# Small-tile matmuls grouped by kind, POOL used throughout, and a new set of plan numbers, in a window-attention and feed-forward kernel

## The chip, the cores and the metric

One NeuronCore of a Trainium2 chip runs the whole kernel. Its engines are TensorE (PE, with its weight loads as PEld), VectorE (DVE), ScalarE (ACT), GpSimd (POOL) and SyncE (SP, which here issues all DMAs). The metric is the device time of one execution in microseconds (us), the median of several runs.

## The reference

Attention with a window of 32 positions and 32 global rows, for 8 batches of 8 heads, and on its output a feed-forward block. Cut to what is computed:

```python
batch, n_heads, seq_l, seq_g, head_dim = (8, 8, 512, 32, 64)
...
s_g = scale * np.matmul(q_g, k_all.transpose(0, 1, 3, 2))
out_g = np.matmul(sm(s_g), v_all)                 # 32 global rows see everything
mask = np.abs(pos[:, None] - pos[None, :]) <= 32
s_ll = np.where(mask, scale * np.matmul(q_l, k_l.transpose(0, 1, 3, 2)), -1000000000.0)
s_l = np.concatenate([scale * np.matmul(q_l, k_g.transpose(0, 1, 3, 2)), s_ll], axis=-1)
out_l = np.matmul(sm(s_l), np.concatenate([v_g, v_l], axis=2))
x = concat(out_g, out_l) as (8 * 544, 512)
h = x @ w_in                                      # 512 -> 2048
sp = np.maximum(h, 0.0) + np.log1p(np.exp(-np.abs(h)))
return ((h * erf(sp)) @ w_out).astype(np.float32)
```

The weights w_in and w_out come as 64-bit floats.

## The kernel before

The kernel doesn't write its instructions in order. It records steps (`add`, with the engines that may take a step, a duration for each, a key, what is read and written, and for PE the number of instructions), and `Program.schedule` lays them out: event by event, each free engine takes from its ready steps the one of lowest key whose buffers are free. The keys are counted in units of the feed-forward work and come from the table of numbers at the head of the file (HKEYS for the heads, GATE, PROJ, KEEP and so on for the rest). The schedule's order is then what each engine runs. Steps marked for DVE and POOL may go to POOL only where their key lies in SHARED; `elsewhere` decides between two engines that may take a step, `crowded` holds back PE steps of many small instructions, and `filler` puts warming matmuls (spare) into PE's row early on where it would be idle.

*Attention.* Heads go in pairs that share q and k. For a pair PE makes the scores of both heads (s, 64 matmuls, tiles of 64x32 in the array); for each head DVE adds the mask and takes row maxima into sm and mx, ACT takes the exponential (for the first BIASED heads with the maximum as its bias, four instructions; later DVE or POOL subtracts it and ACT needs one), PE transposes (t, full 128x128), ACT or DVE copies (pt), PE multiplies with the values (o, 32 matmuls, tiles of 128x32), and DVE divides by the row sum (rs, xn). After a pair, xn is transposed (xT) and stored to DRAM (xsc). After every four heads come the same steps for the 32 global rows (ga, gb scores; pg; gt; go values; gx; xsg). Batch 0 takes a shorter way into the feed-forward block (`straight`, tiles x).

*Feed-forward, first 768 columns.* For each batch c (and chunk 8, the global rows) six units h of 12 matmuls: each product of fp32 numbers is three matmuls of rounded halves (xh with winh, xl with winh, xh with winl). ACT copies h to hs and takes softplus and erf in groups of AG units into sp; DVE or POOL multiplies by hs; gh is the rounded half and gl the rest; PE projects (op, from gh, gl with wouth, woutl) and the partial sums go to DRAM (part). The w_in and w_out blocks are first turned from 64-bit to 32-bit floats by integer steps on DVE (top_in, top_out), and for the other 1,280 columns written back to DRAM (`keep_in`, `keep_unit`: top_l_in, part, top_k_out, hi_k_out, lo_k_out).

*Feed-forward, the other columns.* Batches in pairs: seven block products per unit in place of eight (pa to pd, weights wq), folded by DVE and ACT (u, c, pair), then the same gate and projection, with part added on DVE (os) and the rows stored. The first of these products comes after all attention; behind the last attention step PE has full-array matmuls alone.

In the trace 32 matmuls make one head's values and 64 a pair's scores; all PE matmuls are recorded at line 344 and transposes at 345, ACT at 346, DVE and POOL at 356, and DMAs at 348, since helpers record them.

Of the kernel before, what the change touches and what calls it, by code (L numbers as in the profile page):

```python
# [21 lines left out]
P = 128  # L22
# [7 lines left out]
CROWD, STRETCH, EVADE = 254, 4.013, 0.27  # L30
# [3 lines left out]
HKEYS = ((0, -5.063), (10, -3.503), (22, 0.608), (64, 30.894))  # L34
STEP, GKEY = 0.023, -0.868
QLEAD, VLEAD, RLEAD, XLEAD = 0.459, 0.046, 0.011, 2.412
GOFF, POFF = 1.452, 1.865
WIN, WOUT = (-2.963, -1.41, -1.202), (3.958, 3.604, 3.417)
BIASED, AG = 30, 3
SHARED = (-99.0, 17.961)  # L40
TPAIR = 2.626
KEEP, KSTEP, FIRST = 16.147, 2.595, (-2.849, 0.951)
CVO = (50.84, 53.645, 53.996, 48.864, 55.397)
QLEAD2, XDEL, SLOTS = 10.999, 1.259, 11
GATE1, GATE2, PROJ1, PROJ2 = (3.909, 9.618, 11.922), (13.773, 23.579, 27.539), 17.617, 26.859
SPT = 0.35
BIAS, AHEAD = 1.072, 15.956
# [3 lines left out]
SLACK, PORT = {"PE": 0.8, "SP": 0.8}, 0.7  # L51

# [6 lines left out]
WLEAD = 0.011  # L59
LATER, GFIRST = 8, (-2.568, -2.486)  # L60
NORMAL = 1.125 * 2.0**-15
STRAIGHT, XLATE = True, -0.932
# [44 lines left out]
class Program:  # L107
# [9 lines left out]
    def add(self, ways, key, fn, reads=(), writes=(), moved=0.0, heat=0, ins=None):  # L117
# [9 lines left out]
        op.heat, op.ins = heat, ins or heat // 256  # L127
# [31 lines left out]
    def schedule(self):  # L159
# [28 lines left out]
        warmth, issued = [], []  # L188
# [13 lines left out]
        def fill():  # L202
            dur = fill_dur if now > COLD else 2 * fill_dur
            until["PE"] = max(since, now) + dur
            heapq.heappush(events, (until["PE"], -1, 0, None))
            if now >= since:
                op = Op()
                op.eng, op.ways, op.fn, op.key, op.start, op.heat = "PE", {"PE": dur}, fill_fn, 0.0, now, fill_heat
                op.new, op.bufs = [], []
                order.append(op)  # L210
                warmth.append((now, fill_heat))

# [6 lines left out]
        while events or any(o.eng is None for o in self.ops) and ahead < 1e3:  # L219
# [14 lines left out]
            while picked:  # L234
                picked = False
                for e, q in ready.items():
# [4 lines left out]
                    while until[e] <= now and (dense or q and q[0][0] <= line[front].key + ahead):  # L241
# [4 lines left out]
                        item = dense.pop(0) if dense_only and dense else heapq.heappop(q)  # L246
# [6 lines left out]
                        if any(free[k] < n for k, n in need.items()) or elsewhere(op, e):  # L253
# [22 lines left out]
                        dur = op.ways[e] + toll  # L276
                        if e == "DVE" and op.port:
# [28 lines left out]
def kernel(  # L306
# [109 lines left out]
    def attention(b, h, key):  # L416
# [17 lines left out]
        if h % 2 == 0:  # L434
# [39 lines left out]
        if biased:  # L474
            add({"ACT": 1.05}, key, exps, [TAB, MX], [SM])
# [16 lines left out]
        PT = abuf([P, 4, P], f"pt_{nm}", "pt", 2)  # L492
        add({"PE": 0.5}, key + STEP * 2, transposes, [SM, CS], [T, PT], heat=512, ins=8)
# [3 lines left out]
        def values():  # L497
# [10 lines left out]
        add({"PE": 0.64}, key + STEP * 3, values, [PT, VA, VB], [O], heat=1040, ins=64)  # L508
        RS = abuf([P, 4, 1], f"rs_{nm}", "rs", 2)
        add({"DVE": 0.07},  # L510
            key + STEP * 3,
            lambda: dve.tensor_scalar(RS.ap, O.ap[:, :, D : D + 1], 1e-9, None, op0=ALU.add),
            [O],
            [RS],
        )
        add({"DVE": 0.09}, key + STEP * 3, lambda: dve.reciprocal(RS.ap, RS.ap), [], [RS])

        def norm(e):
            if e == "DVE":
                dve.tensor_tensor(  # L520
                    XN.ap[:, :, r0 : r0 + D], O.ap[:, :, :D], RS.ap.to_broadcast([P, 4, D]), ALU.mult
                )
            else:
                for t in range(4):
                    act(XN.ap[:, t, r0 : r0 + D], O.ap[:, t, :D], AF.Copy, scale=RS.ap[:, t, :])

        add({"DVE": 0.34, "ACT": 0.85}, key + STEP * 3, norm, [O, RS], [XN])
# [20 lines left out]
        if h % 4 == 3:  # L548
# [191 lines left out]
    class View:  # L740
# [3 lines left out]
        def ap(self):  # L744
            return self.f(self.buf.ap)
# [624 lines left out]
```

## Time and profile before

| | before |
|---|---|
| median of 3 runs | 922.99 us (922.47 to 924.45) |
| span of the profiled execution | 920.8 us |
| PE busy | 897.3 us, 97% |
| weight loads (PEld) busy | 720.7 us, 78% |
| DVE busy | 667.2 us, 72% |
| ACT busy | 570.1 us, 62% |
| POOL busy | 61.7 us, 7% |
| HBM traffic | 203 GB/s over the span |

The span runs from the first to the last instruction of the profiled execution; the median of the runs lies 2.2 us above it. Busy times are of engines that overlap each other. A matmul's recorded duration overlaps that of the next, so the pace of PE is read from the starts of successive groups in the chain of waits. The page's share of the chain by line gives op 38%, h 12%, and pa to pd together some 21%.

### The profile page before, as it was taken

The numbers are of one execution on the slowest core, as the hardware profiler recorded it, in microseconds if no ns is written. First come the engines' busy times: TensorE is split into PE (matmuls) and PEld (weight loads), VectorE is DVE, ScalarE is ACT, GpSimd is POOL, SyncE is SP. The second block draws the span as 40 slices with busy tenths as digits, with TensorE's granted clock in tenths as the row PEclk, the third lists the DMA queues.
The fourth block names the chain that finished last, engine by engine and source line by source line (L and its number), as shares of the span: only waits on it lengthen the run. The fifth ranks groups of instructions, "written<-read, shape, count | busy, mean of one in ns | idle before, by whom it ended". The sixth has DMA issues, their size and how long they took to land.

```text
span 920.8 us, 22337 instructions
## 1 busy us (share of the span) xinstructions
PE 897.3 (97%) x8814; PEld 720.7 (78%) x8814; DVE 667.2 (72%) x1733; ACT 570.1 (62%) x975; POOL 61.7 (7%) x51
## 2 busy tenths in 40 slices
PE   8799989999999999999999999999999999999998
PEld 5576767777777778888888888888888888888886
DVE  4698989978979897768857867648674677445562
ACT  4578986656757676866855569425862476335760
POOL 0003543131100000000000000000000000000000
PEclk9899999999999999999999999999999999999999
DMA  9698986979697885823458953644355535455121
GB/s 338 224 305 265 317 270 214 301 240 285 213 313 252 274 281 177 293 110 124 151 204 299 343 181 124 217 139 154 89 183 173 193 91 159 126 170 167 66 80 68
DMA packets 110017, 188.23 MB, mean 204 GB/s; under 512 B 15576, under 2 KB 39384, under 8 KB 109912
## 3 DMA queue, kind: packets, MB, share of 16 engines
q1 hardware_dynamic: 109912, 186.79, 61.8%
q8 instruction: 70, 1.15, 0.5%
q14 instruction: 35, 0.29, 0.1%
HBM read 145.59 MB, written 41.16 MB: 203 GB/s over the span
## 4 chain that ended last, share of the span: by engine, by line
PE 84%; DMA 6%; DVE 6%; issue 2%; ACT 1%; SPq 1%; DVEq 0%; ACTq 0%
PE op L344 38%; PE h L344 12%; PE pd L344 6%; PE pc L344 6%; PE pa L344 6%; PE pb L344 3%; PE o L344 3%; PE t L345 3%; PE s L344 2%; DMA wq<-part 2%; PE h_g L344 2%; DMA vb<-in_vB_dram 1%; DMA xsc<-xT 1%; DMA k<-in_kE_dram 1%; PE gt L345 1%
## 5 line engine op out<-in xcount | busy, mean ns | idle before, releaser
L344 PE MATMUL op<-wouth,gh 128*128 128x512 f32 x544 | 215.9, 397 | 0.4 <-DVE mx L356 0.4
L344 PE MATMUL op<-wouth,gl 128*128 128x512 f32 x544 | 212.1, 390 | 0.2 <-issue 0.2
L344 PE MATMUL op<-woutl,gh 128*128 128x512 f32 x544 | 212.0, 390 | 0.0
L347 ACT ACT_TABLE_LOAD x108 | 138.6, 1283 | 2.7 <-PEq L1357 0.7
L344 PEld LDWEIGHTS op<-wouth,gh 128*128 128x128 f32 x544 | 102.2, 188 | 23.2 <-issue 2.0
L344 PEld LDWEIGHTS op<-wouth,gl 128*128 128x128 f32 x544 | 102.1, 188 | 21.8
L344 PEld LDWEIGHTS op<-woutl,gh 128*128 128x128 f32 x544 | 102.2, 188 | 19.6
L356 DVE TENSOR_TENSOR gl<-sp,gh 128x512 fp32r<-128x512 f32 x129 | 89.4, 707 | 27.8 <-ACT gh L346 18.3
L346 ACT ACTIVATE gh<-sp 128x512 fp32r<-128x512 f32 x94 | 57.2, 627 | 83.8 <-PE op L344 71.1
L344 PE MATMUL h<-xh,winh 128*128 128x512 f32 (+1 forms) x216 | 85.8, 397 | 0.3 <-ACT hs L346 0.3
L344 PE MATMUL h<-xh,winl 128*128 128x512 f32 (+1 forms) x216 | 82.5, 382 | 0.0
L344 PE MATMUL h<-xl,winh 128*128 128x512 f32 (+1 forms) x216 | 82.5, 382 | 0.0
L346 ACT ACTIVATE sp<-sp 128x512 f32<-128x512 f32 x136 | 75.9, 621 | 0.5
L356 DVE CUSTOM_DVE_ANT_0 sm<-s,cs 128x128 f32<-128x128 f32 x256 | 57.1, 283 | 12.2 <-DMA cs<-in_cst_dram 7.0
L344 PE MATMUL pa<-xh_B,wq 128*128 128x512 f32 x160 | 55.8, 389 | 0.0
L344 PE MATMUL pd<-xh_T,wq 128*128 128x512 f32 x160 | 55.6, 389 | 0.0
L346 ACT ACTIVATE hs<-h 128x512 f32<-128x512 f32 x44 | 26.0, 595 | 41.5 <-PE h L344 41.3
L344 PEld LDWEIGHTS h<-xh,winh 128*128 128x128 f32 x216 | 41.1, 190 | 9.3 <-issue 1.0
L356 DVE TENSOR_TENSOR pair<-u,pc 128x512 f32<-128x512 f32 x40 | 27.4, 684 | 27.6 <-PE pc L344 27.5
L344 PEld LDWEIGHTS h<-xh,winl 128*128 128x128 f32 x216 | 41.0, 190 | 8.0
L344 PEld LDWEIGHTS o<-va,pt 128*32 128x32 f32 x768 | 31.7, 109 | 19.1 <-issue 11.2
L344 PEld LDWEIGHTS h<-xl,winh 128*128 128x128 f32 x216 | 41.1, 190 | 6.7
(163 smaller groups left out, 1687.0 us busy)
## 6 DMA issues: line engine op xcount, KB each, us to landing
wq<-wq SPq DMA_DIRECT2D x140, 256.0 KB, 3.3
vb<-in_vB_dram SPq DMA_DIRECT2D x64, 325.0 KB, 5.2
rx<-xsc SPq DMA_DIRECT2D x30, 512.0 KB, 5.4
va<-in_vA_dram SPq DMA_DIRECT2D x64, 195.0 KB, 4.8
k<-in_kE_dram SPq DMA_DIRECT2D x32, 384.0 KB, 5.1
wq<-part SPq DMA_DIRECT2D x35, 256.0 KB, 4.3
q<-in_qT_dram SPq DMA_DIRECT2D x32, 272.0 KB, 4.9
part<-os SPq DMA_DIRECT2D x34, 256.0 KB, 3.4
```

The source lines that it names most:

```text
L344: pe = lambda n, *a, **k: pinned(nc.tensor.matmul(n, *a, **k))
L345: tr = lambda *a, **k: pinned(nc.tensor.transpose(*a, **k))
L346: act = lambda *a, **k: pinned(nc.scalar.activation(*a, **k))
L347: table = lambda name: pinned(nc.scalar.preload_act_table_set(name))
L356: return lambda *a, **k: pinned(f(*a, **k))
```

## The change

The diff gives `schedule` a notion of PE's form: every PE step has a mode (F for full tiles, S for scores, O for values), a change of mode adds a duration from TURN to the plan, and a PE that is in a small form picks the ready step of lowest key after taking NEAR off the keys of its own form. From head 18 on (PAIRED) the two heads' values are one step; from batch 6 on (GOJOIN, GSJOIN) the global values join the pair's values and the global scores join the scores of the second pair. SM and PT get four buffers in place of two. `normalize`, `global_scores`, `global_probs` and `global_rows` hold the former lines of `attention` and `attention_global`. SHARED ends at 151.646, beyond every key. BIASED goes from 30 to 44. Nearly all numbers of the table and many of the planned durations are new. Cut to its core:

```diff
-CROWD, STRETCH, EVADE = 254, 4.013, 0.27
+CROWD, STRETCH, EVADE = 254, 4.013, 0.46
-HKEYS = ((0, -5.063), (10, -3.503), (22, 0.608), (64, 30.894))
-STEP, GKEY = 0.023, -0.868
+HKEYS = ((0, -4.696), (12, -2.264), (22, 0.416), (64, 28.821))
+STEP, GKEY = -0.256, -4.361
...
-BIASED, AG = 30, 3
-SHARED = (-99.0, 17.961)
+BIASED, AG = 44, 3
+SHARED = (-99.0, 151.646)
...
-QLEAD2, XDEL, SLOTS = 10.999, 1.259, 11
+QLEAD2, XDEL, SLOTS = 4.0, -0.178, 10
...
+TURN = {"FS": 0.11, "FO": 0.11, "SF": 0.35, "OF": 0.28, "SO": 0.31, "OS": 0.30}
+NEAR = 2.684
+PAIRED, GOJOIN, GSJOIN, PTS = 17, 6, 6, 4
+SMS, SPARED = 4, 0
...
-STRAIGHT, XLATE = True, -0.932
+STRAIGHT, XLATE = True, 15.301
...
+                        elif e == "PE" and mode != "F" and NEAR:
+                            item = min(q, key=lambda i: (i[0] - (NEAR if i[2].mode == mode else 0.0), i[1]))
+                            q.remove(item)
+                            heapq.heapify(q)
...
+                        if e == "PE":
+                            dur += TURN.get(mode + op.mode, 0.0)
+                            mode = op.mode
...
-            add({"PE": 1.24}, key, scores, [Q, K], SS, heat=2048, ins=128)
+            if h % 4 == 2 and b >= GSJOIN:
+                GA, GB, more = global_scores(b, h // 4, [st["qk", 0], (Q, K)])
+                G0[b, h // 4] = GA, GB
+
+                def joint():
+                    scores()
+                    more()
+
+                add({"PE": 1.9}, key, joint, [*st["qk", 0], Q, K], [*SS, GA, GB, GTURN], heat=3136, ins=160, mode="S")
+            else:
+                add({"PE": 1.02}, key, scores, [Q, K], SS, heat=2048, ins=128, mode="S")
-        SM = abuf([P, 4, P], f"sm_{nm}", "s", 2)
+        SM = abuf([P, 4, P], f"sm_{nm}", "s", SMS)
...
-        PT = abuf([P, 4, P], f"pt_{nm}", "pt", 2)
+        PT = abuf([P, 4, P], f"pt_{nm}", "pt", PTS)
...
+        if h % 4 == 3 and b >= GOJOIN:
+            joined = global_probs(*group, key + GKEY)
+        if NH * b + h - h % 2 < PAIRED:
+            add({"PE": 0.55}, key + STEP * 3, values, [PT, VA, VB], [O], heat=1040, ins=64, mode="O")
+            normalize(O, XN, r0, nm, key)
+        elif h % 2 == 0:
+            st["o"] = values, [PT, VA, VB], O, r0, nm
+        else:
+            first, need, O0, *rest = st["o"]
+            last, more, GO = joined or (None, [], None)
+
+            def pair():
+                first()
+                values()
+                if last:
+                    last()
+
+            add({"PE": 1.11 + 0.72 * (GO is not None)},
+                key + STEP * 3,
+                pair,
+                [*need, PT, VA, VB, *more],
+                [O0, O] + [GO] * (GO is not None),
+                heat=2080,
+                ins=128 + 96 * (GO is not None),
+                mode="O",
+            )
```

On PE, at the values of heads 6 and 7 of batch 6 (o_6_6 and o_6_7; op is a projection), before:

```order
L344 MATMUL o_6_6_5942<-vb_6_6_5814,pt_6_6_5875 32x65 x2
L344 MATMUL o_6_6_5942<-va_6_6_5460,pt_6_6_5875 32x65
L344 MATMUL op_0_3_3_5966<-wouth_0_0_2461,gh_0_3_0_5089 128x512
L344 MATMUL op_0_3_3_5966<-woutl_0_0_2829,gh_0_3_0_5089 128x512
L344 MATMUL op_0_3_3_5966<-wouth_0_0_2461,gl_0_3_0_5174 128x512
L344 MATMUL op_0_3_3_5966<-wouth_0_0_2461,gh_0_3_1_5113 128x512
L344 MATMUL op_0_3_3_5966<-woutl_0_0_2829,gh_0_3_1_5113 128x512
L344 MATMUL op_0_3_3_5966<-wouth_0_0_2461,gl_0_3_1_5194 128x512
L344 MATMUL o_6_7_5985<-va_6_7_5660,pt_6_7_5882 32x65
L344 MATMUL o_6_7_5985<-vb_6_7_5853,pt_6_7_5882 32x65 x2
```

The same place on PE after the change, from the last rows of the unit ahead to the second head's first:

```order
L363 MATMUL o_6_6_6016<-va_6_6_5651,pt_6_6_5924 32x65
L363 MATMUL o_6_7_6017<-va_6_7_5658,pt_6_7_5955 32x65
L363 MATMUL o_6_7_6017<-vb_6_7_5788,pt_6_7_5955 32x65 x2
L363 MATMUL o_6_7_6017<-va_6_7_5658,pt_6_7_5955 32x65
L363 MATMUL o_6_7_6017<-vb_6_7_5788,pt_6_7_5955 32x65 x2
```

Six projection matmuls that stood between the two heads are gone from there; the global values go_6_1 follow the second head at once.

On PE, at the global scores of the first four heads of batch 6 (ga_6_0, gb_6_0; o_5_7 the values before them), before:

```order
L344 MATMUL o_5_7_5150<-vb_5_7_4880,pt_5_7_5092 32x65 x2
L344 MATMUL o_5_7_5150<-va_5_7_4734,pt_5_7_5092 32x65
L344 MATMUL ga_6_0_5177<-k_6_0_4794,q_6_0_4790 32x480 x2
L344 MATMUL ga_6_0_5177<-k_6_2_5009,q_6_2_5007 32x480 x2
L344 MATMUL gb_6_0_5178<-k_6_0_4794,q_6_0_4790 32x64 x2
L344 MATMUL gb_6_0_5178<-k_6_2_5009,q_6_2_5007 32x64 x2
L344 MATMUL op_0_2_3_5067<-wouth_0_1_1953,gh_0_2_2_4145 128x512
```

And after the change, where s_6_2 are the scores of the second pair and h the next unit:

```order
L363 MATMUL s_6_2_0_5175<-k_6_2_4842,q_6_2_4838 32x128 x4
L363 MATMUL s_6_2_1_5176<-k_6_2_4842,q_6_2_4838 32x128 x4
L363 MATMUL ga_6_0_5177<-k_6_0_4624,q_6_0_4590 32x480 x2
L363 MATMUL ga_6_0_5177<-k_6_2_4842,q_6_2_4838 32x480 x2
L363 MATMUL gb_6_0_5178<-k_6_0_4624,q_6_0_4590 32x64 x2
L363 MATMUL gb_6_0_5178<-k_6_2_4842,q_6_2_4838 32x64 x2
L363 MATMUL h_0_3_3_5237<-xh_0_3_0_3264,winh_0_1_940 128x512
```

The global scores have moved from behind values (another small form) to behind the scores of the second pair, with which they now form one step.

On POOL, the last tensor rows of the whole program before (sm is a subtraction of the maximum, xl the rest of a split):

```order
L356 TENSOR_TENSOR sm_4_6_4015<-sm_4_6_4015,mx_4_6_4016 128x512
L356 TENSOR_TENSOR xl_0_3_1_4322<-rx_0_3_1_3565,xh_0_3_1_4292 128x512 x2
L356 TENSOR_TENSOR sm_5_2_4479<-sm_5_2_4479,mx_5_2_4480 128x512
L356 TENSOR_TENSOR sm_5_3_4485<-sm_5_3_4485,mx_5_3_4486 128x512
L356 TENSOR_TENSOR sm_5_4_4689<-sm_5_4_4689,mx_5_4_4690 128x512
L356 TENSOR_TENSOR sm_5_6_5001<-sm_5_6_5001,mx_5_6_5002 128x512
```

POOL after the change, in the same part of the attention stage (part and top_l_in are of the weights kept for later):

```order
L375 TENSOR_TENSOR sm_6_3_5270<-sm_6_3_5270,mx_6_3_5271 128x512
L375 TENSOR_TENSOR part_1_6_5286<-top_l_in_1_1_4638,part_1_6_5286 128x256
L375 TENSOR_TENSOR sp_0_3_0_5221<-sp_0_3_0_5221,hs_0_3_0_4872 128x512
L375 TENSOR_TENSOR sp_0_3_2_5223<-sp_0_3_2_5223,hs_0_3_2_5219 128x512
L375 TENSOR_TENSOR gl_0_3_0_5372<-sp_0_3_0_5221,gh_0_3_0_5355 128x512
L375 TENSOR_TENSOR lo_k_out_1_1_5401<-top_k_out_1_1_5306,hi_k_out_1_1_4918 128x512
L375 TENSOR_TENSOR part_2_0_5510<-top_l_in_2_0_5410,part_2_0_5510 128x256
L375 TENSOR_TENSOR sm_6_5_5513<-sm_6_5_5513,mx_6_5_5514 128x512
```

POOL now takes gates, splits and kept weights there that stood on DVE, and goes on into the stage without attention.

## Rows read from the trace of the kernel before

**Rows 1.** The page: busy tenths of three engines in 40 equal slices of the span.

```profile
PE   8799989999999999999999999999999999999998
...
DVE  4698989978979897768857867648674677445562
...
POOL 0003543131100000000000000000000000000000
```

**Rows 2.** By stretch: busy us (xcount) of PE, PEld, DVE, ACT, POOL; PEclk, DMA share, GB/s.

```profile
0.00:58.00 58.00, 49.37 (x1178) 32.56 (x1178) 37.44 (x179) 32.34 (x86) 3.49 (x7) 0.94 0.82 289
58.00:362.00 304.00, 292.66 (x5098) 224.85 (x5099) 271.19 (x957) 217.14 (x418) 58.22 (x44) 0.99 0.82 264
362.00:850.00 488.00, 488.00 (x2206) 406.28 (x2206) 324.12 (x539) 284.56 (x426) 0.00 (x0) 1.00 0.53 175
```

**Rows 3.** The chain of waits, dense stage: start us, us, what.

```profile
380.00 5.44 PE op L344 x24
```

**Rows 4.** The chain of waits, 245 to 331 us.

```profile
246.60 0.94 PE ga L344 x8
...
247.65 1.59 PE op L344 x6
...
312.10 0.59 PE o L344 x32
312.69 1.59 PE op L344 x6
...
316.68 1.09 PE s L344 x64
...
320.70 0.94 PE ga L344 x8
...
322.71 2.95 PE op L344 x12
...
329.28 1.04 PE o L344 x64
```

**Rows 5.** The start: chain of waits, SP's waits, one stretch of 10 us.

```profile
12.09 0.65 PE spare L344 x3
...
29.20 3.52 issue
...
58.47 1.45 PE h L344 x6
...
SPq L348 <- ACT xT L346: 10.5, 1, 10.5
...
30.00:40.00 10.00, 7.28 (x146) 5.48 (x147) 4.97 (x24) 4.62 (x12) 0.00 (x0) 0.66 0.28 104
```

**Rows 6.** DVE beside POOL: chain, POOL's timeline, PE's wait, groups of masks.

```profile
127.34 1.70 DVE top_out L356
...
129.07 1.64 DVE top_out L356
...
131.11 0.60 DVE top_out L356
...
127.19 2.97 POOL L356 TENSOR_TENSOR sp<-sp,hs 128x512 f32<-128x512 f32 x2 [4.47 <-ACT sp L346]
...
PE gx L344 <- DVE xg L356: 3.4, 1, 3.4
...
L356 DVE CUSTOM_DVE_ANT_0 sm<-s,cs 128x128 f32<-128x128 f32 x256 | 57.1, 283 | 12.2 <-DMA cs<-in_cst_dram 7.0
```

**Rows 7.** Three stretches of 10 us in which DVE is full (columns as rows 2).

```profile
140.00:150.00 10.00, 9.37 (x160) 6.94 (x158) 9.90 (x30) 9.60 (x17) 7.58 (x6) 1.00 0.84 277
150.00:160.00 10.00, 8.96 (x133) 7.19 (x133) 9.86 (x29) 3.93 (x8) 0.30 (x1) 1.00 0.44 128
280.00:290.00 10.00, 9.61 (x161) 7.47 (x141) 9.93 (x37) 9.21 (x14) 0.00 (x0) 1.00 0.98 331
```

**Rows 8.** The page: DMA issues, KB each, median us to landing.

```profile
wq<-wq SPq DMA_DIRECT2D x140, 256.0 KB, 3.3
```

More of the change, by code (lines that the diff above doesn't have):

```diff
@@ L506, in values @@
                 )
[L508 to L527, printed above, removed]
+        group = b, h // 4, [st["va", i] for i in range(h % 4 + 1)], [st["qk", i] for i in range(h % 4 // 2 + 1)]
+        joined = None
+        if h % 4 == 3 and b >= GOJOIN:
[5 more added lines that the diff above has]
+            st["o"] = values, [PT, VA, VB], O, r0, nm
+        else:
+            first, need, O0, *rest = st["o"]
[14 more added lines that the diff above has]
+            )
+            normalize(O0, XN, *rest, key)
+            normalize(O, XN, r0, nm, key)
+            if joined:
+                global_rows(*group[:2], GO, key + GKEY)
         if h % 2 == 1:
@@ L547, in attention @@
                 add({"SP": 4 * SPT}, key + STEP * 4, store, [XT, ATTN], [XSC[b, p]], moved=262.0)
-        if h % 4 == 3:
-            more = b, h // 4, [st["va", i] for i in range(4)], [st["qk", i] for i in range(2)]
+        if h % 4 == 3 and not joined:
             if b == 0 and LATER:
-                held.append((*more, GFIRST[h // 4]))
+                held.append((*group, GFIRST[h // 4]))
             else:
-                attention_global(*more, key + GKEY)
+                attention_global(*group, key + GKEY)
         if NH * b + h == LATER:
@@ L835, in sum_of @@
             add(
-                {"DVE": 0.4, "POOL": 0.8},
+                {"DVE": 0.34, "POOL": 0.8},
                 k,
@@ L941, in gate @@
         add(
-            {"ACT": 2.57 + 1.29 * (ps == 0) + 1.09 * len(us)},
+            {"ACT": 2.6 + 1.31 * (ps == 0) + 1.11 * len(us)},
             key,
@@ L954, in gate @@
             add(
-                {"DVE": 0.75, "POOL": 1.5},
+                {"DVE": 0.62, "POOL": 1.5},
                 k,
@@ L960, in gate @@
             )
-            add({"DVE": 0.43, "ACT": 0.55}, k, lambda e, SPb=SPb, GH=GH: copy(e, GH.ap, SPb.ap), [SPb, *after], [GH, *turn])
+            add({"DVE": 0.36, "ACT": 0.54}, k, lambda e, SPb=SPb, GH=GH: copy(e, GH.ap, SPb.ap), [SPb, *after], [GH, *turn])
             add(
-                {"DVE": 0.75, "POOL": 1.5},
+                {"DVE": 0.62, "POOL": 1.5},
                 k,
@@ L1111, in lo @@
                     )
-            add({"DVE": 0.95, "ACT": 1.1}, k, hi, [A, ATTN], [HI])
-            add({"POOL": 2.8, "DVE": 1.55}, k, lo, [A, HI, ATTN], [LO])
+            add({"DVE": 0.72, "ACT": 1.08}, k, hi, [A, ATTN], [HI])
+            add({"POOL": 2.8, "DVE": 1.23}, k, lo, [A, HI, ATTN], [LO])
             blocks[name] = (HI, LO)
@@ L1118, in sum_of @@
             add(
-                {"DVE": 1.2, "POOL": 2.5},
+                {"DVE": 1.15, "POOL": 2.5},
                 k,
```

94 lines of the change are left out of this document (65 added, 29 removed).

## The prediction

> **What bounds the kernel now.** I read the page's slices first: PE's row is at eight or nine tenths from the third slice on, DVE's at seven to nine from there to the sixteenth, and POOL's ends with the eleventh [rows 1]. Then the stretches [rows 2]. From 362 to 850 us PE is busy 488.00 of 488.00 us: in this dense stage nothing waits for DVE, ACT or a load, and its length is the number of products alone. The chain of waits shows the price of a product there, 24 matmuls in 5.44 us, 0.2267 each [rows 3]. The idle time lies ahead of 362: 8.6 us in the first 58 us (58.00 less 49.37), and 11.3 in the 304 us after it (304.00 less 292.66), where DVE is busy 271.19 of 304, which leaves it 32.8 us, and the DMA engines 0.82 of the time. So two things can shorten the kernel: less PE time in the first 362 us, or less idle time there. Counted through PE's row, 2,346 matmuls of 512 columns and 192 of 256 stand behind the last attention matmul, by 0.2267 and about 0.12 us some 555 us, and 362 + 555 is where the last matmul ends, bar the tail of 3.7 us. Whatever ends the attention stage earlier, for the same products done, ends the kernel earlier by as much.
>
> PE's busy share hides a cost: attention uses small tiles of the array (64x32 for scores, 128x32 for values), the rest 128x128, and each change costs PE time that counts as busy. Two heads' values cut into a projection show it. Six matmuls of op take 1.59 us between excursions where six dense ones take 1.36, so going out costs 0.23; one head's 32 matmuls take 0.59, two heads' 64 together 1.04, so the second head costs 0.45 and the way back 0.14 [rows 3, 4]. An excursion costs 0.37 us beside its work. Scores agree: alone, global scores take from 246.60 to 247.65, 1.05 us, and a pair's scores 1.09; where they happen to follow each other both take from 320.70 to 322.71, 2.01, which saves 0.13 and one way out of 0.23 [rows 4].
>
> **The change, part by part.** *Fewer changes of tile.* Values of two heads become one step from head 18 on, with the global values in it in batches 6 and 7, the global scores join a pair's scores there, and the planner prefers a step of the form that PE is in. Counted through PE's whole row, excursions go from 83 to 62 and changes between the two small forms inside one from 23 to 8. 21 x 0.37 = 7.8, and 15 x 0.14 (the way out of a small form) = 2.1: **9.9 us less**. Four of the excursions saved and five of the inner changes stand ahead of the first h, where PE waits for loads anyway; without them it is 17 x 0.37 + 10 x 0.14 = 7.7. So between 7.7 and 9.9; I take the upper end, since the first h comes earlier (next).
>
> *The start.* The row holds 41 warming matmuls (spare) for 54; three take 0.65 us [rows 5], so 13 are **2.8 us less**, or nothing if PE idles in their place. The first two blocks of w_in now load right behind cs, and the two stores of xT that had SP's queue wait 10.5 us for ACT stand behind eight more loads [rows 5]. In that hole DMA ran at 104 GB/s, PE waited 3.52 us in one place and its granted clock in 30 to 40 was 0.66 of full speed, the lower of the two levels for most of that time [rows 5]. The first h then came at 58.47. In the new row, 35 us of PE work precede the first h for 46 before, by the prices above. The loads at the head of the queue cost the second pair of heads 1 MB of queue, at the 289 GB/s of [rows 2] 3.6 us. Bounds: nothing gained, and all 8.6 us of idle. I take **3 us less**, nearer the lower end because of those 3.6.
>
> *POOL.* SHARED goes from 17.961 to 151.646, so POOL may take DVE's elementwise work to the end: 46 such operations become 210, 108 of them up to the last subtraction of a maximum (head 63), 62 more in the attention stage. DVE isn't relieved by that: it takes copies from ACT (pt 12 to 28, gt 9 to 21, hs 9 to 29, 48 more of some 0.6 us). And a POOL operation slows DVE. Two steps of DVE on whole SBUF tiles (SCALAR_TENSOR_TENSOR, top_out) took 1.70 and 1.64 us while POOL multiplied two tiles in 2.97, where the next instruction of the kind, without POOL, took 0.60 [rows 6]: about 1.05 us of DVE for each POOL operation. PE waited 3.4 us behind it, for xg [rows 6]. The other end is nothing: DVE's mask steps, which read PSUM, take 283 ns on average over all 256 [rows 6]. The Trainium skill, page "SBUF — State Buffer", section "Who interferes with whom", says which DVE instructions collide: those with two SBUF inputs against a GpSimd instruction that reads SBUF, the later one blocked until the earlier ends. By that rule the worst case is a whole POOL operation of some 1.3 us each, 80 us of DVE for 62. The two steps in [rows 6] bear the rule out, in that DVE lost over two thirds of POOL's time. I take half of 1.05, since about half of DVE's work in the stage reads PSUM: 62 x 0.52 = 32 us, which is all the idle time that DVE has there. What PE then loses is read from the slices where DVE is that full (9.86 to 9.93 of 10): PE is at 9.37, 8.96 and 9.61, so 0.7 lost in 10 [rows 7], 21 us over 304 against 11.3 now. So between nothing and 10 us more. Deeper buffers work against it (SM and PT go from 2 to 4, so scores and transposes may run two heads further ahead). I take **3 us more**.
>
> *The dense stage.* Here 102 POOL operations are added where none ran. I take nothing: DVE is busy 324 of 488 us [rows 2], and 102 x 1.05 = 107 us would still fit. The shortest way in PE work from the last matmul of a unit to the first use of its gh is 20 us in the new row and 17 before, and a weight block has 12 us from its slot's release to its use for 13 before (10 slots for 11) where a load lands in 3.3 [rows 8]. Lost cover would show as PE idle behind 367.
>
> *Loads.* From the loads for head 31 to those for head 63, SP's row holds 58.5 MB (tile sizes added up) for 51.2, since more of the second half's weights are turned in this stage. The stage ran at 264 GB/s and a share of 0.82 [rows 2], so by 58.5/51.2 it becomes 302 and 0.94. PE still ran at 9.61 of 10 at a share of 0.98 [rows 7]. It is in the upper end of the range, not in the sum.
>
> The durations of DVE and ACT in the diff's costs change nothing but the plan, and are in the counts.
>
> **The sum.** 9.9 + 2.8 + 3.0 - 3.0 = 12.7 us less than the profiled 920.8: 908.1 us of span. The median of the runs, 922.99, lies 2.2 above that execution's span, so 910.3. The other way to count: 78 dense products (17.7 us) move ahead of the last attention matmul, leaving 537 us behind it, so that matmul should end at 367.
>
> **Rivals.** *Idle falls too.* The deeper buffers and the earlier h take away most of the 8.6 us at the start and half of the 11.3 after: 920.8 - 9.9 - 2.8 - 7 - 5 + 2.2 = 898. For it: the single hole of SP's queue. Against: DVE's 0.89 share. *The changes saved were hidden.* If DVE sets the pace from 58 to 362, PE's saved 7.7 us turn into waits and only the start's gain is left, and with 3 us of collisions it is 920. For it: PE already loses time wherever DVE is full [rows 7]. Against: over half of the stage PE is the one that doesn't wait (292.66 of 304). *Slower: POOL overfills DVE.* At 1.05 us for each of the 62 operations DVE needs 65 us where it has 32.8, so the stage grows by 32: 923 - 12.7 - 3 + 32 = 939. By the skill's rule quoted above it would be 47 rather than 32, so 954. It beats the savings once a POOL operation costs DVE more than about (32.8 + 16)/62 = 0.8 us on average. For it: the 3.4 us wait in [rows 6]. Against: of the 46 operations now, few leave such a trace, since much of DVE's work beside them reads PSUM.
>
> **Chances.** The forecast, 904 to 916: 0.55. Idle falls too: 0.17. Hidden changes and load pressure, 916 to 921: 0.10; to within 0.2%, about what a measurement of this kernel can tell from no change, 0.06. Slower: 0.12. The range from 898 to 923 leaves out a tenth or so on the slow side and some hundredths on the other. Faster 0.82, same 0.06, slower 0.12.
>
> **What would show it.** Right: o in blocks of 64 matmuls and 112, op in sixes rarely at 1.59, the last attention matmul near 367, PE fully busy behind it, spare x41. The first h near 46 to 52 instead of 58.47, with no SP wait for xT near 10 us. DVE's two-input SBUF operations lengthened in the attention stage, and DVE's share there above 0.95. Wrong: the last attention matmul later than 380 (POOL or the loads), PE idle behind it by more than 2 us (gates late because of POOL), or excursions that cost as much in pairs as alone.

## The result, and the profile after

The changed kernel takes 930.96 us (median of 5 runs, 928.81 to 932.19), the kernel before 922.78 beside it: a ratio of 1.0094 with a 95% interval of 1.0069 to 1.0119. It is **slower by 0.9%**, where 1.4% faster was forecast. Its profiled execution has a span of 929.2 us.

The page after, its first line and the slices [rows 1]:

```profile
span 929.2 us, 22486 instructions
...
PE   9888999999989999999999999999999999999998
...
DVE  6698999788889899679726497458755686544543
...
POOL 0011462142535455356313063123304032110320
```

Busy time by stretch (columns as [rows 2]), the attention stage cut where it was cut before, then up to its new end, then the dense stage:

```profile
58.00:362.00 304.00, 282.95 (x4976) 220.48 (x4965) 270.62 (x908) 213.28 (x452) 122.33 (x105) 0.98 0.84 273
362.00:386.00 24.00, 24.00 (x277) 19.66 (x276) 21.44 (x58) 15.76 (x27) 11.35 (x11) 1.00 0.46 147
386.00:850.00 464.00, 462.21 (x2070) 383.06 (x2070) 300.15 (x412) 251.49 (x368) 130.80 (x82) 1.00 0.52 167
```

The last attention matmul ends at 385.3 us, for 362.0 before and 367 forecast. PE idles 21.1 us from 58 to 362 (304.00 less 282.95), for 11.3 before. DVE's busy time there is the same, 270.62 for 271.19, though it runs 908 instructions for 957: each is longer. In the changed kernel PE's matmuls are recorded at line 363, transposes at 364, ACT at 365, DVE and POOL at 375; a run's own edit can shift these by some lines. PE's waits, from the longer ones of this view (who waited, for whom; total, count, longest):

```profile
PE gt L364 <- DVE xn L375: 4.4, 1, 4.4
PE ga L363 <- DMA k<-in_kE_dram: 3.7, 3, 1.9
...
PE gx L363 <- DVE rs L375: 2.0, 1, 2.0
```

The chain of waits at the longest of them (start, us, what), and POOL's timeline beside it:

```profile
262.27 1.10 DVE lo_k_out L375
263.38 1.48 DVE top_k_out L375
...
264.88 1.69 DVE top_k_out L375
...
266.60 1.63 DVE top_k_out L375
...
268.83 0.60 DVE top_k_out L375
...
270.43 0.41 DVE xn L375
...
270.98 0.88 PE gt L364 x3
271.85 4.87 PE h L363 x12
```

```profile
262.79 3.22 POOL L375 TENSOR_TENSOR sp<-sp,hs 128x512 f32<-128x512 f32 x2
265.98 1.70 POOL L375 TENSOR_TENSOR gl<-sp,gh 128x512 fp32r<-128x512 f32 x1
```

Three top_k_out steps take 4.8 us, and POOL is busy beside them without a gap to 267.68; the next one, at 268.83, takes 0.60. xn, which frees the bank that gt writes, stands behind them. PE then waits 4.4 us, and its next 12 products take 4.87 us where 12 take 2.72 at [rows 3]'s pace. The same place by stretches of 5 us shows why: the granted clock is 0.50 of full speed behind the wait, the lower of its two levels (1.2 GHz).

```profile
265.00:270.00 5.00, 1.58 (x6) 0.96 (x6) 4.95 (x7) 1.33 (x4) 2.68 (x2) 0.95 0.24 79
270.00:275.00 5.00, 4.03 (x11) 3.35 (x12) 3.58 (x7) 2.36 (x8) 1.27 (x1) 0.50 1.01 385
275.00:280.00 5.00, 5.00 (x76) 4.04 (x82) 2.84 (x6) 2.83 (x5) 0.00 (x0) 0.87 0.28 86
```

A **ledger** puts all of it in one place. From the starts of all PE matmuls up to the last attention matmul I took off the steady price of each (0.2267 us a product, 0.11 a transpose, 0.22 a spare, the small ones by their pace inside a block) and of each change of tile (0.09 on the last product ahead, 0.15 on the way back, 0.11 on the first product behind, as single steps show them). What remains, here called R, is waits and slow clock.

| us | before | after | difference |
|---|---|---|---|
| products ahead of the last attention matmul | 159.1 | 176.8 | +17.7 |
| warming matmuls | 11.9 | 9.0 | -2.9 |
| changes of tile (83 and 23; 62 and 8) | 30.4 | 21.6 | -8.8 |
| R | 34.6 | 51.8 | +17.2 |
| last attention matmul ends | 362.0 | 385.3 | +23.3 |
| from there to the last matmul | 555.2 | 540.3 | -14.9 |

(The attention's own matmuls are the same in both and left out.) R by stretch: 0 to 60 us 14.4 before and 14.7 after; 60 to 120, 4.8 and 10.1; 120 to 140, 6.6 and 2.0; 140 to 240, 5.3 and 10.3; 240 to 300, 2.6 and 11.9; behind 300, about 1 and 3.

### The profile page after: what moved, and what is told of

Same layout as the page of the kernel before. It is cut to its first block, busy times and chain, and to the rows that moved or that the text cites. A ratio compares the mean times of both kernels' runs of the same rounds, so it can differ in the third digit from the quotient of the medians.

```text
span 929.2 us, 22486 instructions
## 1 busy us (share of the span) xinstructions
PE 896.3 (96%) x8801; PEld 722.5 (78%) x8801; DVE 666.0 (72%) x1607; ACT 554.9 (60%) x991; POOL 281.7 (30%) x215
## 4 chain that ended last, share of the span: by engine, by line
PE 69%; DVE 14%; DMA 10%; issue 3%; SPq 2%; ACT 1%; POOL 1%; DVEq 0%; ACTq 0%; POOLq 0%
PE op L363 32%; PE h L363 8%; PE pd L363 6%; PE pc L363 6%; PE pa L363 6%; PE pb L363 3%; DMA wq<-part 2%; DMA xsc<-xT 2%; SPq L367 2%; DMA va<-in_vA_dram 2%; DVE sm L375 2%; DVE top_k_out L375 2%; PE o L363 2%; PE h_g L363 2%; PE s L363 1%
## 5 line engine op out<-in xcount | busy, mean ns | idle before, releaser
L365 ACT ACTIVATE gh<-sp 128x512 fp32r<-128x512 f32 x80 | 48.6, 628 | 119.0 <-PE op L363 104.3
L375 DVE TENSOR_TENSOR gl<-sp,gh 128x512 fp32r<-128x512 f32 x96 | 85.6, 901 | 7.1 <-ACT gh L365 2.6
L375 POOL TENSOR_TENSOR gl<-sp,gh 128x512 fp32r<-128x512 f32 x40 | 60.5, 1518 | 49.1 <-DVE gh L375 24.2
L375 DVE CAST gh<-sp 128x512 fp32r<-128x512 f32 x56 | 30.1, 540 | 52.2 <-PE op L363 52.1
L375 POOL TENSOR_TENSOR sp<-sp,pair 128x512 f32<-128x512 f32 x18 | 24.5, 1379 | 131.4 <-ACT sp L365 131.4
L365 ACT ACTIVATE sm<-sm,mx 128x128 f32<-128x128 f32 x176 | 54.7, 394 | 10.6 <-DVE mx L375 10.5
L375 POOL TENSOR_TENSOR sp<-sp,hs 128x512 f32<-128x512 f32 x32 | 45.3, 1429 | 39.7 <-ACT sp L365 39.7
L375 DVE TENSOR_TENSOR pair<-u,pc 128x512 f32<-128x512 f32 x40 | 27.4, 685 | 31.3 <-PE pc L363 31.3
```

The lines of the kernel that those rows point to most:

```text
L365: act = lambda *a, **k: pinned(nc.scalar.activation(*a, **k))
L375: return lambda *a, **k: pinned(f(*a, **k))
```

## Experiments

In most of them the plan is made as in the changed kernel and then kept, row for row; only what a step does, or which engine does it, differs. So a difference isn't that of another plan. Below, "end" is that of the last attention matmul, "behind" the time from there to the last matmul.

| run | median us | ratio to before, 95% | end | behind | R |
|---|---|---|---|---|---|
| changed kernel | 930.96 | 1.0094 (1.0069 to 1.0119) | 385.3 | 540.3 | 51.8 |
| e1 POOL light | 915.92 | 0.9912 (0.9884 to 0.9941) | 373.0 | 537.5 | 39.7 |
| e2 DVE does it | 929.29 | 1.0068 (1.0044 to 1.0092) | 386.9 | 537.5 | 53.6 |
| e3 scores later | 932.32 | 1.0099 (1.0070 to 1.0128) | 386.2 | 540.3 | 53.1 |
| e4 pairs cut | 941.22 | 1.0189 (1.0157 to 1.0221) | 395.5 | 541.0 | 55.2 |
| e5 copies back | 933.57 | 1.0119 (1.0096 to 1.0141) | 388.1 | 539.4 | 54.6 |
| e6 POOL writes | 916.11 | 0.9939 (0.9918 to 0.9959) | 373.3 | 537.5 | 39.9 |
| e7 more loads | 937.21 | 1.0154 (1.0127 to 1.0180) | 392.0 | 540.3 | 58.5 |
| e8 before, POOL light | 918.10 | 0.9950 (0.9932 to 0.9967) | 359.2 | 555.2 | 31.7 |
| e9 fewer loads | 932.67 | 1.0110 (1.0081 to 1.0139) | 386.4 | 540.3 | 52.9 |
| e10 before, fewer loads | 923.41 | 1.0003 (0.9981 to 1.0024) | 362.7 | 555.2 | 35.2 |
| e11 before, joined | 931.75 | 1.0102 (1.0072 to 1.0132) | 371.3 | 555.2 | 47.2 |
| e12 e6, fewer loads | 917.77 | 0.9941 (0.9923 to 0.9960) | 376.3 | 537.5 | 42.8 |
| e13 e6, light top | 913.59 | 0.9908 (0.9885 to 0.9931) | 370.4 | 537.5 | 36.9 |
| e14 joins undone | 935.22 | 1.0155 (1.0127 to 1.0183) | 361.0 | 569.3 | 53.0 |
| e15 before, DVE does it | 922.64 | 1.0013 (0.9996 to 1.0030) | 362.9 | 555.2 | 35.4 |
| e16 e13, fewer loads | 912.39 | 0.9876 (0.9841 to 0.9910) | 370.5 | 537.5 | 37.0 |
| e17 two xT | 931.09 | 1.0085 (1.0054 to 1.0116) | 389.8 | 540.3 | 56.3 |
| e18 before, two xT | 922.49 | 0.9997 (0.9978 to 1.0016) | 361.4 | 555.2 | 34.0 |

In the traces of e1 to e4 the records of five warming matmuls are missing (36 for 41, while the matmuls around them start as in the other runs); their 1.1 us is taken off R here. Single profiles differ by some us in "end" (e17's, 4.5 us later than the changed kernel's, is of its slowest execution, 935.42); the medians carry the verdicts.

### POOL: its work, its lateness, or its reads

**e1** lets POOL's later operations do next to nothing:

```diff
...
+        light = op.eng == "POOL" and len(op.ways) > 1 and op.key >= 17.961
-        op.fn(*([op.eng] if len(op.ways) > 1 else []))
+        op.fn(*(["LIGHT" if light else op.eng] if len(op.ways) > 1 else []))
```

> The changed kernel with its plan unchanged, row for row, except that the 164 tensor operations that POOL has gained (key of 17.961 or more) do next to nothing: those that work in place touch 32 of 512 columns, the others write zeros without reading. So part of the computation is left out; every step, wait and order stays. Theory A (POOL's reads lengthen DVE's steps, DVE's queue is late, and PE waits and then runs at the lower clock): the waits of PE at 266, 289 and 433 to 446 us and the low clock behind the first two go, about 10 to 12 us, so 919 to 921. Theory B (the time was lost to loads of k that global scores wait for too early, and to nothing that POOL does): 931 less at most 2.

The key covers 190 of POOL's 210 operations, more than the 164 expected. Measured 915.92, 15.0 us less than the changed kernel and beyond the 10 to 12 of theory A; theory B falls as the main cause.

**e2** hands the same operations to DVE:

```diff
+        eng = "DVE" if op.eng == "POOL" and op.key >= 17.961 else op.eng
+        op.fn(*([eng] if len(op.ways) > 1 else []))
```

> The changed kernel with its plan unchanged, but the same 164 operations run on DVE, at the place in its order that the plan's times give. Adds 164 x 0.65 = 107 us of DVE work and takes away the lengthening beside POOL (some 77 us over the whole kernel by DVE's busy time). Theory A, if lengthening is as bad as the work itself: about even in the attention stage, 928 to 934. Theory A, if what hurts is only the bunching of long steps ahead of PE's waits: 920 to 925. If POOL does relieve DVE after all: 940 or more.

Measured 929.29, near even. The columns of the table split it: behind the attention it regains all of the 2.8 us, ahead of it the end comes 1.6 later. For the kernel's time it is the same whether DVE does the work or is slowed by POOL doing it, though DVE's busy time is 18 us longer when it does (684.4 for 666.0).

**e6** keeps POOL busy as long, but without reads:

```diff
...
+            for _ in range(2 if math.prod(dst.shape[1:]) == 256 else 3):
+                pool.memset(dst.bitcast(F32), 0.0)
...
```

> The changed kernel with its plan unchanged, but the POOL operations with a key of 17.961 or more (190 by the last trace) are replaced by two or three writes of zeros over the same tile, about as long (3 x 0.55 us for 512 columns, 2 x 0.33 for 256), which read nothing from SBUF. So part of the computation is left out. In the run with light POOL, DVE's steps beside such writes kept their length. Theory A2 (the collision of reads is what costs): as with POOL made light, 915 to 919. Rival (POOL's results come late, 1.4 us where DVE would take 0.65): 925 to 931.

Measured 916.11, as light POOL. So POOL's time costs nothing, its **reads of SBUF beside DVE's** do. Lateness is taken out only in part: 67 of the 190 operations write another tile than those they read, and there the write doesn't wait for the inputs (gl in e6 waits for the product that read it last, not for gh), so that those results come early. What speaks against lateness is the changed kernel's own trace: no wait of PE names POOL, and POOL has 1% of the chain that ended last, where DVE has 14%. DVE's and POOL's timelines at the place shown above, now 4 us earlier:

```profile
259.35 0.69 DVE L375 TENSOR_TENSOR lo_k_out<-top_k_out,hi_k_out 128x512 fp32r<-128x512 f32 x1
259.95 0.42 DVE L375 TENSOR_SCALAR top_k_out<-raw_k_out 128x512 int32<-128x512 int32 x1
260.41 1.42 DVE L375 SCALAR_TENSOR_TENSOR top_k_out<-raw_k_out,top_k_out 128x512 int32<-128x512 int32 x2
```

```profile
259.72 0.90 POOL L375 MEMSET part<- 128x256 f32 x2
260.57 3.34 POOL L375 MEMSET sp<- 128x512 f32 x6
```

The same three steps of top_k_out take 1.8 us for 4.8, beside a POOL that is just as busy. No slow clock follows (the same two stretches of 5 us; the granted clock is the third number from the end):

```profile
265.00:270.00 5.00, 5.00 (x30) 4.34 (x30) 3.13 (x6) 4.33 (x12) 2.27 (x4) 1.00 1.03 384
270.00:275.00 5.00, 5.00 (x82) 3.85 (x81) 4.93 (x23) 2.81 (x6) 1.68 (x4) 1.00 0.59 123
```

DVE's busy time falls from 666.0 to 596.3 us, 70 us, or 0.37 for each of the 190. It isn't spread evenly: by the durations of DVE's instructions added up, 0.20 for each of the 98 ahead of the attention's end (408.1 less 388.7) and 0.56 for each of the 92 behind it (354.3 less 303.2); against e1, whose writes are shorter, 0.29 and 0.60. The Trainium skill, page "SBUF — State Buffer", section "Who interferes with whom", states just this: a DVE instruction with two SBUF inputs contends with a GpSimd instruction that reads SBUF, not with one that only writes it. The runs agree with it: with POOL reading, TENSOR_TENSOR of 128x512 took up to 2.90 us on DVE, in e6 never more than 0.69. But one of the three steps above, the TENSOR_SCALAR, reads a single tile and was lengthened as well, 1.48 for 0.42; the last section comes back to that.

**e8** does to the kernel before what e1 does to the changed one, for all its 46 operations (the same diff, without the key).

> The kernel before with its plan unchanged, but its 46 POOL operations made light (in place: 32 of 512 columns; the others write zeros). So part of the computation is left out. Theory A: its 20 us of lengthened DVE steps go, and with them the 3.3 us wait of PE at 129 us and the low clock behind it: 3 to 6 us less, 917 to 920. If POOL's price comes only with the many operations of the new plan: 922 to 923.

Measured 918.10, some 4 us less: the old plan paid for POOL too, though the operations were few. So of the 15 us, 11 are the change's. **e15** gives the 46 to DVE (the diff of e2, without the key).

> The kernel before with its plan unchanged, but its 46 POOL operations run on DVE, at their place by the plan's times: 30 us of DVE work more, 20 us of lengthening less, in a stage where DVE is idle 33 of 304 us. If a POOL operation is worth nothing, as the same exchange in the changed kernel had it: 920 to 923. If POOL relieves DVE in the old plan: 926 or more.

Measured 922.64: POOL is worth nothing in the old plan either, and DVE in its place gains nothing.

### What the changes of tile are worth

**e4** cuts the joined pairs again, with the product that followed put between the halves; `later` moves a step behind the next n of PE, and with it whatever depends on it:

```diff
+    for op in [o for o in order if hasattr(o, "two")]:
+        i = order.index(op)
...
+        head.eng, head.ways, head.fn, head.key, head.mode = "PE", op.ways, op.two[0], op.key, "O"
+        head.new, head.bufs, head.outs, op.new = op.new, op.bufs, [], []
+        op.fn = op.two[1]
+        order.insert(i, head)
+        later(order, [((op,), 1)])
```

> The changed kernel with its plan unchanged, but each joined pair of values that a full-tile product follows is cut again, with that product between its halves: excursions of PE into small tiles go from 60 to 81 by its row (the part ahead counts the same row), all else is kept. If an excursion costs 0.34 to 0.37 us of PE time and PE sets the pace: 7 to 8 us more, 938 to 939. If the saved changes were hidden behind other waits in the attention stage: 931 to 933.

Measured 941.22, 10.3 us more. The ledger counts 20 more excursions, 6.8 us at its own price of 0.34 each, and 3.4 us more of R. So PE does set the pace, and a cut costs at least the price of the excursion; the 3.4 us beside it fit results that come later, which no run separates.

**e14** undoes the joins alone, and is planned anew:

```diff
-PAIRED, GOJOIN, GSJOIN, PTS = 17, 6, 6, 4
+PAIRED, GOJOIN, GSJOIN, PTS = 64, 8, 8, 4
```

> The changed kernel with its joins alone undone (values of two heads, global values, global scores are steps of their own), all keys and the preference for PE's own form kept, and planned anew. By its row 73 excursions for 60 and 20 inner changes for 9. At 0.34 and 0.15 us: 6 us more, 937, if joining has no price. If joined steps come late enough to cost what they save: 929 to 932. Below 928: joining costs more than it saves.

Measured 935.22, 4.3 more, of 5.8 by its changes of tile (27.4 for 21.6). Joining pays, most of what it promised, as far as a plan made anew can tell (642 products stand ahead of its last attention matmul for 780).

**e11** joins in the kernel before, by putting 17 steps off until a step of their form comes:

```diff
+        for n in range(1, reach + 1):
+            if FORM.get(kind(row[i + 1 + n])) == FORM[kind(op)]:
...
+                later(order, [((op,), n)])
+            if kind(row[i + 1 + n]) in FORM:
+                break
...
+    join(order, 2, ("o", "go", "ga"))
```

> The kernel before with its plan kept, except that 17 steps of values, global values and global scores are put off by one or two steps of PE, so that they stand directly ahead of a step of the same form: excursions into small tiles 80 to 73 and changes inside them 23 to 17 by PE's row (counted without the few that the trace shows more). POOL, loads and all other rows as before. At 0.34 us an excursion and 0.15 an inner change 3.3 us less: 919 to 920, if nothing that waited for these steps is on the path. If their later results cost as much: 922 to 923.

Measured 931.75. Its changes cost 3.4 us less as expected, and R grew by 12.6, nearly four times that. Only the order of steps differs, so results that come one or two steps of PE later are what costs; which of the 17 cost it, no run shows. Here a join was worth its price only where the plan was made for it.

### The other waits

With POOL's later reads taken out of the changed kernel (e6, 916.1) and all of them out of the old one (e8, 918.1), it is only 2.0 us faster, though its changes of tile and warming matmuls cost 11.7 less. R holds the difference, 39.9 for 31.7, most of it from 60 to 120 us: 10.6 for 4.4. PE's busy time in that stretch, before, after and in e6:

```profile
60.00:120.00 60.00, 57.18 (x1152) 43.28 (x1151) 55.16 (x210) 52.86 (x121) 22.45 (x17) 1.00 0.89 290
...
60.00:120.00 60.00, 53.30 (x1242) 40.91 (x1242) 55.37 (x236) 50.86 (x140) 15.22 (x12) 1.00 0.90 289
...
60.00:120.00 60.00, 54.22 (x1236) 41.15 (x1237) 55.16 (x233) 49.88 (x135) 15.21 (x11) 1.00 0.90 282
```

The new plan starts the scores of eight pairs there, the old one of six. Ten runs looked for the resource that this overfills. One suspect stays in all of them: the POOL operations up to 123 us have keys below 17.961 and read as before, in e6 too. The trace speaks against it: some 8 of the 10 us of R in that stretch stand ahead of 100 us, and DVE's steps that lost more than 0.25 us there, four with 3.2 us in all, come at 101 us and later. **e3** moves global scores that waited for k, and the scores behind them, past the next product:

```diff
+    later(order, ((("ga_2_1", "s_2_6_0"), 1), (("ga_5_0", "s_5_0_0"), 1), (("ga_5_1", "s_5_4_0"), 1)))
```

> The changed kernel with its plan unchanged, except that at three places (global scores of the second half of batch 2, of both halves of batch 5) the global scores and the pair's scores behind them change places with the 6-matmul product that follows, so that the load of k has 1.36 us longer each time. PE waited 3.7 us there for k by the waits, about 5.4 by its pace. Theory B: 3 to 4 us less, 927 to 928. Theory A: the same 931, within 1.5, as the time is lost later to DVE anyway.

The edit did what it should, and the time stayed (932.32). PE's waits in it show where it went, to waits for DVE, the longest new one for gn, which belongs to the global scores:

```profile
PE op L400 <- DVE gn L412: 2.8, 1, 2.8
...
PE ga L400 <- DMA k<-in_kE_dram: 0.5, 1, 0.5
```

**e7** adds transfers, **e9** and **e10** take six loads away, in the changed kernel and in the one before:

```diff
+        for n, (K, src) in enumerate(TWICE):        # e7: k of batches 2 and 3
+            if op.new and op.new[0] is K:
+                dma(again[n], src)
...
+        if name[:4] == "out_":                      # e9, e10
+            add({"SP": SPT}, key - lead, lambda: pool.memset(RAW.ap.bitcast(F32), 1.0), deps, [RAW, TOP.buf, ABS.buf] if lead == RLEAD else [RAW], moved=524)
```

> The changed kernel with its plan unchanged, and behind each load of k of batches 2 and 3 (8 loads, issued between 56 and 107 us) one more transfer of the same 377 KB from DRAM to a DRAM tile that nobody reads: 3.0 MB, 10.4 us at the 289 GB/s of that stretch. Theory C (from 60 to 120 us the loads set the pace, so that what PE saves there and the earlier first h come to nothing): 6 to 10 us more, 937 to 941. If the waits there have another cause: 931 to 934.

> The changed kernel with its plan unchanged, but the six loads of the first half's w_out (512 KB each; five are issued between 60 and 130 us) are replaced by POOL writing a constant over the tile, so that part of the weights is left out: 2.6 MB, 9 us at the 289 GB/s of that stretch. Counted as PE's time beyond its matmuls, changes of tile and warming, the stretch 60 to 120 us holds 10.1 us of waits in the changed kernel for 4.8 before. Theory C (loads set the pace there): those waits fall to about 5, and the time to 925 to 927. If they have another cause: 930 to 932.

> The same six loads replaced in the kernel before, its plan unchanged. Its waits from 60 to 120 us are 4.8 us. Theory C, if the loads matter only for the new plan, which runs its heads earlier there: 921 to 923. If both plans wait for loads alike: 917 to 919.

More loads cost 6.3 us (937.21), of the 10.4 that they take; fewer gain nothing (932.67 and 923.41). In e9 PE no longer waits for k at length, but 2.7 us for a copy instead:

```profile
PE s L363 <- DVE pt L375: 2.7, 1, 2.7
```

**e5** gives 63 copies back to ACT, in the changed kernel as it is:

```diff
+        back = op.eng == "DVE" and set(op.ways) == {"ACT", "DVE"} and op.bufs[-1].name in BACK
+        op.fn(*(["ACT" if back else op.eng] if len(op.ways) > 1 else []))
```

> The changed kernel with its plan unchanged, but 63 copies out of PSUM (24 hs, 23 pt, 16 gt) that the new plan gives to DVE and the old one gave to ACT run on ACT, each at its place by the plan's times. Takes 63 x 0.62 = 39 us off DVE and gives ACT some 35. Theory A1 (DVE's queue is too full in the attention stage, whatever fills it): PE's waits for rs, xn and xg shrink as in the run with POOL made light, 918 to 924. Theory A2 (only DVE steps lengthened by POOL count): the lengthening stays, 926 to 931. If ACT's queue becomes the late one: 932 or more.

Measured 933.57, the last of the three cases: PE now waits 6.6 us for copies on ACT (3.4 ahead of t, 3.2 ahead of gb) for which it didn't wait in the changed kernel. So the time doesn't say what relieving DVE is worth. What the trace does show is that with 39 us less of DVE work the longest wait of gt is still there at its full length (4.5 us), and so are the lengthened steps ahead of it (1.52, 1.68 and 1.63 us): for that wait it isn't how full DVE is that counts. **e12**, **e13** and **e16** remove loads (as e9), DVE work, and both, from e6; the DVE part of e13 is, for one of the three steps,

```diff
+            few = 32 if name.startswith(("in_", "out_")) else 512
...
-            dve.scalar_tensor_tensor(top, word(0), 29, top, op0=ALU.logical_shift_right, op1=ALU.bitwise_or)
...
+            dve.scalar_tensor_tensor(
+                top[:, :few], word(0)[:, :few], 29, top[:, :few], op0=ALU.logical_shift_right, op1=ALU.bitwise_or
+            )
```

and the same for the two others.

> The changed kernel with its plan unchanged, with both suspects removed: POOL's later operations replaced by writes as long (as in the run that gave 916) and the six loads of w_out replaced as above. Part of the computation is left out. If collisions and loads are the whole of what the forecast missed, the time comes near the forecast's sum without its POOL term, 907 to 911. If the loads don't matter, 916 again.

> The run with POOL's later operations replaced by writes as long (916), and besides three of DVE's in-place steps on each of the 12 tiles of the first half's weights (top_in, top_out) work on 32 of 512 columns: some 22 us of DVE less between 20 and 150 us. Part of the computation is left out. Theory D (the new plan puts eight pairs' scores between 60 and 120 us where the old one puts six, and DVE, which spends 55 of those 60 us, can't feed them): the waits of that stretch fall from 10.6 us to 5 or less, and the time to 909 to 911. Rival (the heads' chain of steps is too long there whatever DVE's load, or its loads): 914 to 917.

> The run with POOL's later operations as writes and DVE's steps on the first weights made light (913.6), and besides the six loads of w_out replaced by a constant: both suspects for the stretch 60 to 120 us are taken away together, where each alone left its 10 to 11 us of waits. Part of the computation is left out. If loads and DVE take turns there as the later one: waits of 6 us or less and 907 to 910. If something else sets that stretch (the chain of steps from a pair's scores to its values): 912 to 915.

Loads alone: 917.77, nothing. Some 16 us of DVE work besides (busy 579.9 us for 596.3, where 22 were expected): 913.59, 2.5 less, but R from 60 to 120 us stays at 11.3. Both: 912.39, 1.2 below e13 and within the spread of the runs, and PE's idle time there is 5.8 us (60.00 less 54.20), as in e6 (60.00 less 54.22). **e17** and **e18** give xT, for whose store DVE waited in that stretch in the new plan alone, a second buffer (`bufs=b.bufs + (b.tag == "xT")`).

> The changed kernel with its plan unchanged, but two buffers for xT in place of one. From 60 to 120 us DVE waited three times, 1.4 us in all, for the last store of xT to land (8 pairs there in place of 6 before), and SP's loads of k and va stand behind stores that wait for xT. Theory E (the turn-round of xT is the third limit of that stretch): its waits fall from 10.1 us by 2 to 4, and the time to 927 to 929. Otherwise 930 to 932.

> The kernel before with its plan unchanged and two buffers for xT. DVE shows no wait for the landing of a store there between 60 and 120 us. Theory E: 922 to 923, as the old plan leaves xT time; if xT holds the old plan up too, 918 to 921.

Measured 931.09 and 922.49: nothing in either. So these 5 to 6 us **stay open**. None of the three suspects accounts for them alone: loads and DVE's load were lightened, xT's buffer doubled, and other waits took the place. That eight pairs are simply too many for the length of the chain of steps from scores to values there fits, but no run tested it, since a plan with other keys for the heads differs everywhere.

No run that computes the whole beats the kernel before.

## Why the prediction failed

The forecast's span was 908.1, the profiled one 929.2: 21.1 us apart. By the forecast's own steps:

- *The bound, and what ends the kernel*: right. The dense stage runs at its pace (537.5 us behind the last attention matmul wherever POOL's reads are gone, 537 counted), 78 products moved ahead of it, and the end follows the attention's end. The mark "later than 380" named POOL or the loads; it was POOL.
- *Fewer changes of tile*, 9.9: right, 8.8 by the ledger, 0.34 an excursion for 0.37, and e4 and e14 show that they are on the path. 1.1 us of the miss.
- *Warming matmuls*, 2.8: right, 2.9.
- *The start*, 3 less: it came to nothing. The first h is at 39.3 us for 58.47 and PE's idle time to 58 fell by 2.2, but the 13 warming matmuls that went had stood in the same holes, and R to 60 us is 14.7 for 14.4. So the step seems to have counted one gain twice. 3 us of the miss.
- *POOL*, 3 more: the step that failed. Priced by e6, POOL's reads cost 12.0 us ahead of the attention's end (385.3 for 373.3) and 2.8 behind it; the old plan paid 2.8 by the same measure (362.0 for 359.2 in e8). So 9 us are new in the attention stage, where 3 were put: 6 us of the miss. The failing part is not the price of an operation, which was taken too high: 0.52 us of DVE, and 0.2 to 0.3 measured in that stage. It is the way from there to PE: I spread the lengthening evenly, found DVE full, and read PE's loss from slices where DVE is full. DVE's share never rose (270.62 us for 271.19, where over 0.95 was named as the sign), because POOL took away about as much work as its reads added (908 instructions for 957 in the same time). What PE paid came in bunches: three or four lengthened steps in a row ahead of one that frees a bank for it, 4.4 and 2.0 us at 266 and 289 us, and then the lower clock. R from 240 to 300 us is 11.9, and 5.3 without the reads. The rival "POOL overfills DVE" had the sign right and the mechanism half: it was to decide above 0.8 us an operation, and the loss came at 0.2 to 0.3.
- *The dense stage*, nothing: 2.8 us of the miss, at 0.56 us of DVE an operation. The cover named, DVE idle a third of the time, is an average; from 410 to 446 us DVE is busy 35.7 of 36 us, and there its steps beside POOL are among the longest (last section).
- *Idle time otherwise as before*: not argued at all, and wrong. The wait at 129 us [rows 6] did go (R from 120 to 140 us 2.0 for 6.6), and 5.3 us came up from 60 to 120, some more behind. Of R's 17.2, 8.2 are left when POOL's reads are priced out of both plans (39.9 in e6 for 31.7 in e8): 8 us of the miss, the larger part of it from 60 to 120 us, and its cause stays open.
- *Loads*, in the range's upper end only: the runs bear that out, in that taking 2.6 MB away gains nothing (e9), though adding 3.0 MB costs (e7).

Added up, 1 + 3 + 6 + 3 + 8 make the 21. The direction turned on POOL: with its later reads out, the plan takes 916.1 and is faster than the old one, by less than half of what was forecast. The range's upper end, 923, left 12.7 us for all terms together. The new plan's waits elsewhere had no upper bound in it; those that the old one shows in stretches as crowded as [rows 7] would have been one.

## What to carry to other kernels

Don't judge help from POOL by DVE's busy share: look for runs of three or four DVE steps with SBUF inputs ahead of a step that frees a bank or feeds PE, and ask what stands beside them on POOL. A kernel whose plan is tuned tells little by its terms: take a saving as an upper bound (4.3 us of 5.8 in e14), since waits come back elsewhere, and the old kernel's waits are not a floor for the new one. To price a suspect, keep the plan and make the suspect harmless (writes of the same length for reads), and look at what the replacement no longer waits for; taking loads or work away only moved the wait here.

## What the chip showed that I had not expected

A DVE step can lose all that is left of a POOL instruction's time. From the dense stage of the changed kernel, DVE and POOL:

```profile
430.89 2.90 DVE L375 TENSOR_TENSOR gl<-sp,gh 128x512 fp32r<-128x512 f32 x1
...
440.09 4.05 DVE L375 CAST xh<-rx 128x512 fp32r<-128x512 f32 x2
```

```profile
429.92 3.32 POOL L375 TENSOR_TENSOR rt<-rx,rt 128x1024 f32<-128x1024 f32 x1 [4.24 <-DVE xl_T L375]
...
437.88 3.43 POOL L375 TENSOR_TENSOR xl_T<-rt,xh_T 128x512 fp32r<-128x512 f32 x2
441.26 2.58 POOL L375 TENSOR_TENSOR rx<-rx,rt 128x1024 f32<-128x1024 f32 x1
```

gl, 0.69 us beside POOL's writes in e6, takes 2.90 and ends 0.55 behind POOL's 1,024 columns, as if it had stood until they were through. The two casts, one SBUF input each and 0.42 in e8 (the median of its 98), take 4.05 together, so a single input is no shelter. For such steps POOL's writes aren't harmless either: behind 150 us in e6, 22 casts of this size took 0.66 to 0.87. The Trainium skill, page "SBUF — State Buffer", section "Who interferes with whom", has both: the later of two contending instructions blocks wholly, and copies, casts and tensor_scalar can contend as well, in the modes that use both ports. Which mode these casts ran in, no run here shows. The prediction took the sentence on two inputs and left the others.

The slow clock is a price of its own: behind the 4.4 us wait 12 products cost 2.15 us more than at full clock (4.87 less 2.72), and behind the old plan's 3.4 us wait 12 took 4.34, 1.62 more, at a granted clock of 0.89 and 0.77 in the stretches of 5 us from 130. Each of these two waits cost about half of itself again.
